# The first batch's depthwise convolution as five fp32 products on TensorE

## The chip, the cores and the metric

The kernel runs on one core of one Trainium2 chip, as one launch. The metric is the device time of one execution in microseconds; the median of several runs is compared. A core has five engines with an instruction queue each: TensorE (PE; its weight loads are shown as PEld), VectorE (DVE), ScalarE (ACT), GpSimd (POOL) and SyncE (SP).

## The reference

Three blocks follow one another: attention that keeps the 32 largest scores of a row, a gated layer whose gate is a causal depthwise convolution of five taps, and a mixer over tokens and channels. All data are float32.

```python
# attention: B, H, S, D = 4, 8, 576, 64
scores = q @ k.T / sqrt(D)
kth = 32nd largest of each row
attn = softmax(where(scores >= kth, scores, -1e9))
x = attn @ v                          # then to (4, 576, 512)
# gate: five taps a channel
xp = concatenate([zeros(4 rows), x])
gate_pre = sum(conv_w[k] * xp[:, k:k+S, :] for k in range(5))
gate = 1 / (1 + exp(-gate_pre))
x = (gate * (x @ w_val)) @ w_out
# mixer
theta = x @ w_theta
u = x + w_tok_r @ (x * cos(theta)) + w_tok_i @ (x * sin(theta))
out = u + maximum(u @ w_ch, 0)
```

## The kernel before

Channels lie on the 128 partitions and tokens along the free dimension in the gated layer. Two heads make a unit u (16 units: batch b = u // 4, head pair hp = u % 4). Attention works in 144 tiles of 128 query rows against 576 keys. In batch 0 (`SPLIT`) the units are gone through twice: first the query columns 0 to 255 of the four head pairs (x = 0, four tiles each), then columns 256 to 575 (x = 1, five tiles each). A stretch (u, x) is called a part here. In the other batches a unit's nine tiles are contiguous and its convolution is done once over 576 columns.

The main loop (L1317) takes one tile a step. In a step, VectorE picks the largest scores of one tile (`pick`), takes the threshold of an earlier one (`rest`) and masks a still earlier one (`mask`); ScalarE copies scores out of PSUM (`scores_out`), counts (`count`), exponentiates (`expo`) and copies the transposed tile (`turn_out`); GpSimd forms the products that the threshold needs (`below`); TensorE computes scores three tiles ahead (`scores_pe`, `AHEAD` = 3) and transposes (`turn`). VectorE and ScalarE execute in the order in which the program issues (`FIXED`); the framework's scheduler orders TensorE, GpSimd and the DMA queue by priority and readiness.

When the last tile of a part is masked, `close` starts a generator. `follow_up` resumes each such generator twice a step, so two yields are one step. It multiplies by v into `px` (L746), divides by the row sums into `xT` (L764), and then, from L788 on, convolves: tap 0 on ScalarE into g, tap 1 on ScalarE into `ct` and added by GpSimd, taps 2, 3 and 4 as multiply-adds on VectorE, and at last tanh in place (sigmoid is taken as tanh of half the argument). There are six yields between the first tap and tanh.

The gated layer and the mixer are jobs, generators in a list that is worked off in order: `front` (x @ w_val, gate, w_out, theta, sine and cosine) and `back` (token mix `py`, channel mix `ph`). In batch 0 `front` runs once for each half of the columns. Before each product with w_val it waits until the part's tanh is issued (`ready`). In each step `work` gives the jobs a budget in model nanoseconds, `BASE` = 4150; the attention's own TensorE work is taken from the same account `owed`, which can't be saved up beyond one step's amount. Batch 0 multiplies in plain fp32, later batches (`THREE`) in split halves.

PSUM tiles of `px`, the jobs and all that have tag "m" share four buffers (`ps_m`).

Of the kernel before, what the change touches and what calls it, by code (L numbers as in the profile page):

```python
# [11 lines left out]
F32 = mybir.dt.float32  # L12
# [4 lines left out]
AF = mybir.ActivationFunctionType  # L17
ALU = mybir.AluOpType
# [57 lines left out]
@with_exitstack  # L76
def attention_gate_phase_mixer(ctx, tc, *tensors):


    nc = tc.nc  # L80
    keep = ctx.enter_context(tc.tile_pool(name="keep", bufs=1))
    flag = keep.tile([1, 1], F32, name="flag")
    mixer(tc, *tensors, flag)

    over = nc.values_load(flag.bitcast(I32), min_val=0, max_val=0x7F000000,
                          skip_runtime_bounds_check_because="a count of rows")
    with tc.If(over > 0):
        mixer(tc, *tensors, None)
# [3 lines left out]
def mixer(ctx, tc, qT, kT, vt, w_val, conv_t, w_out, w_theta, w_tok, w_ch, out, flag):  # L92
    nc = tc.nc
    safe = flag is None
    P = 128
    B, S, DM = vt.shape
    U = qT.shape[0]
    NP = U // B
# [8 lines left out]
    NC = DM // P  # L107
    KW = conv_t.shape[1]
# [11 lines left out]
    ml = ctx.enter_context(tc.tile_pool(name="ml", bufs=1))  # L120
# [3 lines left out]
    ps_m = ctx.enter_context(tc.tile_pool(name="ps_m", bufs=BANKS[2], space=bass.MemoryType.PSUM))  # L124
# [39 lines left out]
    ident = cp.tile([P, P], F32, name="ident")  # L164
# [19 lines left out]
    raws, heads, there, ready = {}, {}, set(), set()  # L184
    s_tiles, s_psum, groups, xT, gate, W, ms = {}, {}, {}, {}, {}, {}, {}
    owed = [0.0]
# [5 lines left out]
    def tabled(out, src, func, **more):  # L192

        ins = nc.scalar.activation(out, src, func, **more).ins  # L194
        table = func == AF.Sin
        if (not table) in last and TABLED:
            tc.add_manual_dep(ins, last[not table].name, mybir.DependencyInfo(
                mybir.DependencyClass.NoSync, mybir.DependencyReason.DATA), reason="one table at a time")
        last[table] = ins
# [47 lines left out]
    def double(u, j, x):  # L247

        r = slice(64 * j, 64 * j + 64)
        q2 = q2s[j]  # L250
        kh, kl = (io.tile([P, S], I32, tag=f"{t}{j}", name=f"{t}{j}_{u}_{x}") for t in ("kh", "kl"))
        for d in range(2):
            o = slice(64 * d, 64 * d + 64)
            nc.sync.dma_start(kh[o, :], raws["k", u, x][0][r, :].bitcast(I32))
            nc.sync.dma_start(kl[o, :], raws["k", u, x][1][r, :].bitcast(I32))
            q = raws["q", u, x][d][r, :].bitcast(I32)
            c = columns_of("q", x)
            if j and c.stop == S:
                nc.sync.dma_start(q2[o, c.start : NF * P], q[:, c.start : NF * P])
                nc.sync.dma_start(q2[o, S:], q[:, NF * P :])  # L260
            else:
                nc.sync.dma_start(q2[o, c], q[:, c])
        heads[u, j] = tuple(t.bitcast(F32R) for t in (q2, kh, kl))
# [110 lines left out]
    ROOM = (CUT, S - CUT + REM)  # L374
# [303 lines left out]
    def turn_out(i):  # L678
# [5 lines left out]
        else:  # L684
            nc.scalar.copy(pT[:, e.j * NF : e.j * NF + NF, o : o + P], e.pt)  # L685

    def close(part):

        u, x = part["u"], part["x"]
        b, hp = divmod(u, NP)  # L690
        lo, hi = COLS[x]
        w = hi - lo
# [50 lines left out]
        for c in range(NF + 1):  # L743
            for j in range(2):
                r, k = (slice(0, P), j * NF + c) if c < NF else (slice(REM * j, REM * j + REM), 2 * NF)
                nc.tensor.matmul(px[64 * j : 64 * j + 64, :], v[r, c, 64 * j : 64 * j + 64], pT[r, k, :],  # L746
                                 start=(c == 0), stop=(c == NF), skip_group_check=True)
# [18 lines left out]
        split = b in SPLIT  # L766
        if not split and x == 0:
            return
        if split and x:
            g = gate[b][hp]  # L770
        else:
            drain(("gate", (u - GB) // NP))
            g = sp.tile([P, S], F32, tag="gp", name=f"gp_{u}", bufs=GB)
            gate.setdefault(b, []).append(g)
        if not split:
            lo = 0
        g = g[:, lo:hi]
# [7 lines left out]
        while lacking["conv"]:  # L785
            yield
            yield
        taps = [xt[:, k + lo : k + hi] for k in range(KW)]  # L788
        nc.scalar.activation(g, taps[0], AF.Copy, scale=cw[:, hp, 0:1])
        for k in CT:  # L790
            ct = wk.tile([P, S], F32, tag="ct", name=f"ct_{u}_{x}_{k}")[:, : g.shape[1]]
# [372 lines left out]
    for b in range(B):  # L1164
        late = b == B - 1
        f = 1.275 if b in THREE else 1.675
# [49 lines left out]
    for k, part in enumerate(order):  # L1216
        i0 = part["tiles"][0].i
        u, x = part["u"], part["x"]
        split = u // NP in SPLIT
# [4 lines left out]
        elif split or x == 0:  # L1224
            when = (i0 - 7, i0 - 5, i0 - 5, i0 - 4, i0 - 3) if split or i0 and order[k - 1]["x"] and order[k - 1]["u"] // NP in SPLIT else (i0 - 9, i0 - 8, i0 - 7, i0 - 6, i0 - 3)
            a = (u, x if split else None)
            for step, do in zip(when, (load_heads, split_high, split_low, *(
                    lambda u, x, j=j: double(u, j, x) for j in range(2)))):
# [37 lines left out]
    def begin_close(i):  # L1266
        e = seq[i]
        if e is e.part["tiles"][-1]:
            chains.append(close(e.part))
# [103 lines left out]
```

## Time and profile before

| | |
|---|---|
| median of 3 runs (lowest to highest) | 860.22 us (859.59 to 861.25) |
| profiled execution | 861.91 us |
| its span, first to last instruction | 859.8 us |
| busy: PE / DVE / ACT / POOL | 88% / 81% / 75% / 51% |
| mean granted TensorE clock | 0.938 |

The profile describes one execution. Busy times of an engine are shares of its span; a busy TensorE is one that has matmuls in flight, whose ends are modelled. A granted clock of 1.00 is 2.4 GHz, 0.50 is 1.2 GHz. The name before an arrow is what is written, the one behind it what is read; L801 is line 801 of the kernel. Most instructions overlap a neighbour a little at their ends, so start-to-start times are shorter than durations.

### The profile page before, as it was taken

The page shows a single profiled execution, that of the slowest core. Times are in us where ns is not written, and L with a number is a line of the kernel's source. Part 1 is how long each engine was busy: PE and PEld are TensorE (multiplying, and loading weights), DVE is VectorE, ACT ScalarE, POOL GpSimd, SP SyncE. Part 2 cuts the span into 40 slices and gives each one's busy share as a digit, 9 for nine tenths or more (in the row PEclk, how much of TensorE's full clock was granted, in tenths as well). Part 3 has the DMA queues.
Part 4 walks back from the last instruction along what each step waited for, and adds up shares of the span by engine and source line. Part 5 has one row for each costly group of instructions (what it writes and reads, how often), then busy time and mean ns, then how long its engine had stood idle before and what let it go on. Part 6 is the DMA issues. An engine that isn't in the chain of part 4 may idle for free.

```text
span 859.8 us, 15896 instructions
## 1 busy us (share of the span) xinstructions
PE 755.6 (88%) x4526; PEld 574.1 (67%) x4526; DVE 697.2 (81%) x2810; ACT 648.4 (75%) x1589; POOL 442.3 (51%) x579
## 2 busy tenths in 40 slices
PE   4577878958789598989798989999999999999995
PEld 3344556535555377668587677769797776798895
DVE  6999999989999769699988979889998696253522
ACT  6787898888888867697879789779888794436511
POOL 4766565655646335364758634546797143014500
PEclk9996888968999889999999989999999999999998
DMA  6576555634442214224755652222855300061002
GB/s 170 150 194 172 148 156 158 167 92 98 129 119 57 68 45 130 64 57 146 218 155 164 183 141 69 57 68 58 235 142 152 98 2 14 1 191 62 2 2 59
DMA packets 73601, 94.35 MB, mean 110 GB/s; under 512 B 13728, under 2 KB 37152, under 8 KB 73504
## 3 DMA queue, kind: packets, MB, share of 16 engines
q1 hardware_dynamic: 73184, 92.82, 39.8%
q8 instruction: 38, 0.62, 0.3%
q14 instruction: 59, 0.48, 0.2%
q10 hardware_dynamic: 320, 0.43, 0.2%
HBM read 49.96 MB, written 13.11 MB: 73 GB/s over the span
## 4 chain that ended last, share of the span: by engine, by line
PE 46%; DVE 33%; ACT 9%; issue 6%; POOL 4%; DMA 2%; SPq 0%; ACTq 0%; POOLq 0%; DVEq 0%
PE py L1087 10%; PE px L746 7%; DVE cand L573 7%; DVE thrs L600 5%; PE ph L508 5%; PE pth L508 4%; PE pt L666 3%; PE pval L508 3%; DVE gp L801 3%; PE py L1106 3%; DVE s L653 3%; DVE cand L579 3%; DVE tops L577 3%; PE px2t L508 2%; PE ps L537 2%
## 5 line engine op out<-in xcount | busy, mean ns | idle before, releaser
L594 POOL TENSOR_TENSOR y<-s,n 128x576 f32<-128x576 f32 x144 | 189.8, 1318 | 197.0 <-DVE thrs L600 148.2
L573 DVE MAX8 cand<-s 128x8 f32<-128x96 f32 x864 | 210.8, 245 | 0.5 <-ACT s L551 0.5
L653 DVE SCALAR_TENSOR_TENSOR s<-s,thrs,e 128x576 f32<-128x576 f32 x144 | 140.1, 973 | 8.0 <-ACT e L194 8.0
L586 ACT ACTIVATE n<-s,tops 128x576 bf16<-128x576 f32 x144 | 112.1, 778 | 34.2 <-POOL y L595 18.6
L551 ACT ACTIVATE s<-ps 128x256 f32<-128x256 f32 (+1 forms) x288 | 104.0, 406 | 41.3 <-PE ps L719 20.3
L666 PE MATMUL pt<-ident,s 128*128 128x128 f32 x576 | 97.9, 295 | 33.8 <-ACT pT L685 22.2
L746 PE MATMUL px<-pT,v 128*64 128x256 f32 (+3 forms) x640 | 111.5, 444 | 12.7 <-ACT pT L685 12.7
L1087 PE MATMUL py<-w_tok,z 128*128 128x256 f32 (+1 forms) x432 | 120.3, 421 | 1.7 <-DVE z L946 1.7
L600 DVE MAX8 thrs<-y 128x8 f32<-128x584 f32 x144 | 109.4, 759 | 6.3 <-POOL y L595 6.0
L666 PEld LDWEIGHTS pt<-ident,s 128*128 128x128 f32 x576 | 70.0, 148 | 62.8 <-ACT pT L685 32.2
L194 ACT ACTIVATE e<-s,least 128x576 f32<-128x576 f32 x144 | 110.8, 769 | 0.1
L537 PE MATMUL ps<-kh_None,q 128*128 128x256 f32 x240 | 95.9, 406 | 4.9 <-ACT s L551 2.9
L685 ACT COPY pT<-pt 128x512 f32<-128x512 f32 x128 | 73.1, 571 | 30.4 <-PE pt L666 18.6
L1087 PEld LDWEIGHTS py<-w_tok,z 128*128 128x128 f32 x432 | 80.9, 198 | 22.0 <-DVE z L946 2.5
L746 PEld LDWEIGHTS px<-pT,v 128*64 128x64 f32 (+1 forms) x640 | 44.6, 143 | 63.3 <-issue 28.0
L577 DVE MAX8 tops<-cand 128x8 f32<-128x48 f32 x432 | 83.0, 192 | 0.1
L538 PE MATMUL ps<-kl_None,q 128*128 128x256 f32 x240 | 72.9, 306 | 0.0
L537 PEld LDWEIGHTS ps<-kh_None,q 128*128 128x128 f32 x240 | 48.2, 201 | 24.2 <-issue 7.2
L537 PE MATMUL ps<-kh,q 128*128 128x256 f32 (+1 forms) x80 | 39.8, 502 | 19.1 <-ACT s L551 8.9
L579 DVE MATCH_REPLACE8 cand<-tops,cand 128x48 f32<-128x48 f32 x288 | 55.2, 192 | 0.0
L1066 DVE TENSOR_TENSOR x2T<-py,x2T 128x256 f32<-128x256 f32 (+1 forms) x32 | 14.4, 450 | 46.9 <-PE py L1087 27.8
L801 DVE SCALAR_TENSOR_TENSOR gp<-xT,w_conv,gp 128x576 f32<-128x576 f32 (+2 forms) x60 | 46.9, 782 | 6.0 <-POOL gp L793 5.3
(205 smaller groups left out, 1725.4 us busy)
## 6 DMA issues: line engine op xcount, KB each, us to landing
kh_None<-kh_None SPq DMA_DIRECT2D x48, 144.0 KB, 2.6
kl_None<-kl_None SPq DMA_DIRECT2D x48, 144.0 KB, 2.7
v<-in_vt_dram SPq DMA_DIRECT2D x20, 256.0 KB, 3.0
out_dram<-x2T SPq DMA_DIRECT2D x16, 256.0 KB, 3.1
w<-ch SPq DMA_DIRECT2D x16, 256.0 KB, 4.7
w<-theta SPq DMA_DIRECT2D x16, 256.0 KB, 5.1
raw_hi<-in_w_tok_dram SPq DMA_DIRECT2D x14, 256.0 KB, 2.8
kh<-kh SPq DMA_DIRECT2D x24, 144.0 KB, 2.4
```

Of the source, the lines that this page charges most:

```text
L194: ins = nc.scalar.activation(out, src, func, **more).ins
L508: nc.tensor.matmul(ps[o : o + n], x, y, start=(i + k == 0), stop=(i == last and k == len(ways) - 1), skip_group_check=(n < P))
L537: nc.tensor.matmul(bank[:, :w], q2, kh[:, lo:hi], start=(j == js[0]), stop=False)
L573: nc.vector.max(d["cand"][:, k, 8 * x : 8 * x + 8], s_tiles[i][:, x * SUB : (x + 1) * SUB])
L577: nc.vector.max(top, c)
L586: nc.scalar.activation(n, s_tiles[i], AF.Sign, bias=d["tops"][:, k, KC - 1 : KC], scale=-(1.0 + 2.0 ** -22), accum_out=acc)
L594: nc.gpsimd.tensor_tensor(y[:, :S], s_tiles[i], d.pop(("n", k)), ALU.mult)
L600: nc.vector.max(thrs[:, N - 1 - i : N - 1 - i + NK], d.pop(("y", k)))
L653: nc.vector.scalar_tensor_tensor(p, p, thr(i), e.exp, ALU.is_ge, ALU.mult, accum_out=part["sums"][:, e.slot : e.slot + 1])
L666: nc.tensor.transpose(e.pt[:, c, :], p[:, c * P : (c + 1) * P], ident)
L746: nc.tensor.matmul(px[64 * j : 64 * j + 64, :], v[r, c, 64 * j : 64 * j + 64], pT[r, k, :], start=(c == 0), stop=(c == NF), skip_group_che ...
L1087: nc.tensor.matmul(ps, z[:, m * P : (m + 1) * P], W["tok"][:, w, lo:hi], start=(i + k == 0), stop=(i == NF))
```

## The change

In batch 0 alone, each part's convolution becomes five fp32 matmuls that accumulate in one PSUM tile: the stationary operand of tap k is a 128 x 128 diagonal matrix of the tap's weights, the moving operand is `xT` shifted by k. Tanh reads PSUM and writes the gate. GpSimd makes the five diagonal matrices of a head pair in one operation (identity times taps, both broadcast) when a head pair is first met; they lie in a buffer with tag "room1" that batch 0 doesn't use until the second half of its `front`. The planner's account `owed` is charged 1.675 ns a column and tap. Between the matmuls and tanh there are two yields; the function returns before the old code.

```diff
--- before.py
+++ after.py
@@ -683,6 +683,19 @@
                            e.pt.rearrange("p c (j w) -> p j c w", j=2))
         else:
             nc.scalar.copy(pT[:, e.j * NF : e.j * NF + NF, o : o + P], e.pt)
+
+    diagonals = {}
+
+    def diagonal(hp):
+
+        if not diagonals:
+            all_of = ml.tile([P, 2 * NC * ROOM[1]], F32, tag="room1", name="diagonals")
+            diagonals["all"] = all_of[:, : NP * KW * P].rearrange("p (u k w) -> p u k w", u=NP, k=KW)
+        if hp not in diagonals:
+            diagonals[hp] = diagonals["all"][:, hp]
+            nc.gpsimd.tensor_tensor(diagonals[hp], ident.unsqueeze(1).broadcast_to([P, KW, P]),
+                                    W["conv"][:, hp, :].unsqueeze(2).broadcast_to([P, KW, P]), ALU.mult)
+        return diagonals[hp]
 
     def close(part):
 
@@ -786,6 +799,16 @@
             yield
             yield
         taps = [xt[:, k + lo : k + hi] for k in range(KW)]
+        if split:
+            owed[0] -= 1.675 * KW * (hi - lo)
+            ps = ps_m.tile([P, hi - lo], F32, tag="m", name=f"pconv_{u}_{x}")
+            for k in range(KW):
+                nc.tensor.matmul(ps, diagonal(hp)[:, k, :], taps[k], start=(k == 0), stop=(k == KW - 1))
+            yield
+            yield
+            tabled(g, ps, AF.Tanh, scale=0.5)
+            ready.add((u, x))
+            return
         nc.scalar.activation(g, taps[0], AF.Copy, scale=cw[:, hp, 0:1])
         for k in CT:
             ct = wk.tile([P, S], F32, tag="ct", name=f"ct_{u}_{x}_{k}")[:, : g.shape[1]]
```

## Rows read from the trace of the kernel before

**Rows 1.** Stretches, us: busy PE, PEld, DVE, ACT, POOL (instructions); clock; DMA share; GB/s.

```profile
60.00:245.00 185.00, 145.91 (x708) 95.13 (x709) 178.74 (x757) 158.18 (x419) 109.70 (x155) 0.82 0.53 138
245.00:285.00 40.00, 38.18 (x212) 22.96 (x211) 39.72 (x173) 34.53 (x91) 23.78 (x33) 1.00 0.33 81
285.00:302.00 17.00, 9.38 (x59) 5.42 (x60) 12.62 (x54) 16.09 (x32) 4.95 (x8) 0.83 0.35 85
302.00:425.00 123.00, 113.31 (x695) 88.27 (x694) 105.06 (x441) 95.47 (x236) 63.01 (x77) 0.95 0.39 107
425.00:760.00 335.00, 324.60 (x2096) 255.09 (x2097) 271.94 (x1090) 261.39 (x630) 180.02 (x218) 0.98 0.37 103
```

**Rows 2.** Waits of VectorE and ScalarE, 60 to 245 us: total us, times, longest.

```profile
DVE s L653 <- ACT e L194: 3.6, 2, 3.4
DVE xT L764 <- ACT rb L726: 1.1, 1, 1.1
...
ACT pT L685 <- PE px L746: 11.7, 4, 4.0
```

**Rows 3.** Instruction groups, 60 to 245 us: busy us, mean ns, idle before.

```profile
L653 DVE SCALAR_TENSOR_TENSOR s<-s,thrs,e 128x576 f32<-128x576 f32 x37 | 34.6, 935 | 3.6 <-ACT e L194 3.6
...
L801 DVE SCALAR_TENSOR_TENSOR gp<-xT,w_conv,gp 128x320 f32<-128x320 f32 x12 | 7.5, 625 | 0.1
...
L801 DVE SCALAR_TENSOR_TENSOR gp<-xT,w_conv,gp 128x256 f32<-128x256 f32 x12 | 6.7, 558 | 0.1
...
L793 POOL TENSOR_TENSOR gp<-gp,ct 128x320 f32<-128x320 f32 x4 | 3.5, 866 | 0.0
...
L793 POOL TENSOR_TENSOR gp<-gp,ct 128x256 f32<-128x256 f32 x4 | 3.2, 803 | 0.0
...
L789 ACT ACTIVATE gp<-xT,w_conv 128x320 f32<-128x320 f32 x4 | 2.2, 557 | 0.0
...
L789 ACT ACTIVATE gp<-xT,w_conv 128x256 f32<-128x256 f32 x4 | 2.0, 492 | 0.0
```

**Rows 4.** Timeline: a mask alone, and one beside an add on GpSimd.

```profile
61.84 0.81 DVE L653 SCALAR_TENSOR_TENSOR s<-s,thrs,e 128x576 f32<-128x576 f32 x1
...
69.86 0.87 POOL L793 TENSOR_TENSOR gp<-gp,ct 128x256 f32<-128x256 f32 x1
...
70.06 1.28 DVE L653 SCALAR_TENSOR_TENSOR s<-s,thrs,e 128x576 f32<-128x576 f32 x1
```

**Rows 5.** Timeline of TensorE: fp32 products, 256 columns at both clocks, 320 at full.

```profile
102.04 2.32 PE L508 MATMUL pval<-xT,w_val 128*128 128x256 f32 x10
...
146.16 2.76 PE L508 MATMUL px2t<-gp,w_out 128*128 128x256 f32 x6
...
260.95 2.32 PE L508 MATMUL px2t<-gp,w_out 128*128 128x320 f32 x8
```

**Rows 6.** Stretches of 2 us as in the first group, with the granted clock.

```profile
66.00:68.00 2.00, 0.85 (x4) 0.45 (x2) 1.97 (x7) 2.00 (x5) 0.56 (x2) 0.50 0.87 250
...
74.00:76.00 2.00, 1.86 (x16) 0.70 (x12) 2.00 (x15) 0.01 (x1) 1.43 (x2) 0.95 0.35 121
...
146.00:148.00 2.00, 2.00 (x7) 1.64 (x6) 2.00 (x12) 1.96 (x7) 1.20 (x2) 0.50 0.29 60
```

**Rows 7.** Timeline: the last part of batch 0 and the jobs around it.

```profile
189.62 2.48 DVE L946 TENSOR_TENSOR z<-px,z 128x512 f32<-128x512 f32 x4
...
223.38 0.48 DVE L764 TENSOR_TENSOR xT<-px,rb 128x320 f32<-128x320 f32 x1
...
227.80 0.59 ACT L789 ACTIVATE gp<-xT,w_conv 128x320 f32<-128x320 f32 x1
...
244.80 0.46 ACT L194 ACTIVATE gp<-gp 128x320 f32<-128x320 f32 x1
...
248.96 0.45 DVE L830 SCALAR_TENSOR_TENSOR gp<-gp,pval 128x320 f32<-128x320 f32 x1
...
302.25 1.06 PE L1087 MATMUL py<-w_tok,z 128*128 128x256 f32 x2
```

## The prediction

> **What bounds the kernel now.** I read the stage table first [rows 1]: busy time of every engine in five stretches, with the granted clock behind it. Between 60 and 245 us VectorE is busy 178.7 of 185 us (97%), ScalarE 158.2, TensorE only 145.9. From 302 us on it is the other way round: TensorE holds 113.3 of 123 us, then 324.6 of 335, while VectorE falls to about 80%. So there are two regimes: VectorE paces the attention of the first batch, TensorE everything after it. Between them, at 285 to 302, TensorE idles 7.6 of 17 us. All eight convolutions that the diff touches lie in the first regime.
>
> The table of waits [rows 2] confirms it: VectorE has two kinds of wait worth a row in these 185 us, together 4.7 us, of which 3.4 is one mask waiting for an exponential. ScalarE, however, waited 11.7 us in four goes for its transposed tiles, which stood behind the attention products px on TensorE; that did not reach VectorE then, because the kernel computes scores three tiles ahead.
>
> **What is removed.** Per part of 256 or 320 columns there go two copies on ScalarE (L789, L792), one add on GpSimd (L793) and three multiply-adds on VectorE (L801). VectorE: 12 multiply-adds of 256 columns, 6.7 us, and 12 of 320, 7.5 us [rows 3], together 14.2. One part, the second half of head pair 1, lies in 170 to 200 us, where two table loads and the sines sit on ScalarE and VectorE has its only long wait; its three, a quarter of 7.5 = 1.9, I count at nothing. That leaves 12.3 us. ScalarE: four groups of copies, 2.2 + 2.0 for L789 and the same again for L792, 8.4 us; ScalarE has 27 us of room, so at nothing; were it the pace setter, up to 8.4 us more.
>
> **What is added on GpSimd.** Four products of 5 x 128 = 640 elements, one for each head pair. No row has this shape. The adds take 803 ns for 256 and 866 ns for 320 elements [rows 3]; continued along this slope 640 cost 1.2 us, in proportion to the smaller one 2.0. I take 1.6, so 6.4 us, against eight adds removed: 4 x 0.80 + 4 x 0.87 = 6.7. Net nothing. GpSimd is busy 109.7 of 185 us, and the products need only the identity and the taps, so they can fill its gaps; the first matmul of a head pair waits for its product at worst, 1.6 us four times, behind which scores stand that are wanted only three tiles later.
>
> A GpSimd operation can also hold VectorE up: a mask that takes 0.81 us alone took 1.28 beside an add [rows 4], 0.47 us more. Eight such delays leave, four perhaps longer ones come: from -3.8 us to, if each product stops VectorE for its whole length, +6.4. I take 0, since the GpSimd time is equal.
>
> The Trainium skill, SBUF — State Buffer, section "Who interferes with whom", speaks against the new products: VectorE and GpSimd share a port pair under an exclusive lock, and the loser blocks to the end. The 0.47 us agree with it. By the strict rule the sum below would lose up to 6.4 us and stand at about 856; by the equal times it stands as worked out.
>
> **What is added on TensorE.** Five fp32 products a part. An fp32 product leaves two records: 10 records of 256 columns took 2.32 us, 8 of 320 took 2.32 [rows 5], so about 0.21 and 0.27 us each once neighbours overlap, 0.43 and 0.53 a product. (The last of a merged row still drains, so the row divided by its count is a little high.) A part costs 5 x 0.43 = 2.13 or 2.67 us, eight parts 4 x 4.8 = 19.2 us at 2.4 GHz. At 1.2 GHz six records of 256 took 2.76 us [rows 5], twice as much: 38.4 is the upper end. The clock is down in places: 0.50 at 66 to 68 us after thin work, back at 0.95 by 74 to 76 after a stretch of products [rows 6]; the mean of the stage is 0.82, so 19.2 / 0.82 = 23.4 us at today's clock. The idle time there is 185 - 145.9 = 39.1 us [rows 1]. It fits, but TensorE comes to 169.3 of some 173. Lower bound of what this costs: 0, all in gaps; upper: 39.1 us of gaps are there, half of them waits that stay, so up to 23.4 - 19.5 = 4 us beyond the old pace. I take 2 us off the gain, as the row that is nearest (four waits of ScalarE behind px, at most 4.0 us [rows 2]) did not reach VectorE.
>
> The Trainium skill, TensorE: Matmul & The Clock Gate, Part 1, says that the slow clock is the default and activity lifts it. The clock rows agree; by it the added work would cost nearer 19.2 than 23.4 us, which favours the sum as it stands.
>
> **What moves.** The generator yields twice instead of six times between the first tap and tanh. On the last part tanh stands at 244.80 us, 17 us after the first tap at 227.80, and the last gating product at 248.96 waits for it [rows 7]. Two yields are a step of about 5 us (37 masks in 185 us [rows 3]), so tanh comes two steps earlier. Against that, each part takes 2.14 or 2.68 us off the planner's budget `owed`, 19.3 in all, so other jobs are emitted later. I put both at zero together: the first half's jobs reach their last product at 189.62 us and the second half's begin after 223.38 [rows 7], so the debits of most parts fall where nothing waits, and the last one (2.68 us, a step of spare budget) is about what the earlier tanh gives back.
>
> The accumulator takes one of four buffers of `ps_m` until tanh has read it, a step; px behind it could wait for one; that is part of the 2 us above and of C below. Tanh reads PSUM instead of SBUF; no row has that, bounds 0 and a doubling of 8 x 0.46 = 3.7 us on ScalarE, below the 8.4 it sheds.
>
> **Sum.** 12.3 - 2 = 10.3 us. The profiled execution took 861.9 (span 859.8 and 2.1 around it), so 851.6; the median of the runs shown is 860.2, 1.7 lower, so **850** for that. Bounds: with all 14.2 us and 3.8 of port delays and no contention, 842; with 6.4 of port delays and 4 of contention, 860.2 - 12.3 + 10.4 = 858.
>
> **The rivals.** B: the earlier tanh does more. If the second half's chain moves up a step or two, the token mix that starts at 302.25 us [rows 7] fills the 7.6 us that TensorE idles before it, and the TensorE regime starts sooner: 850 - 7.6 = 842. For it speaks that the gate is the last thing waited for; against, the last debit.
>
> C: TensorE becomes the bound of the first regime. 169.3 us of work plus a quarter to a half of the present gaps (9.8 to 19.5) is 179 to 189 us against 185: 854 to 864, middle 859. For it: px already holds ScalarE up by 4.0 us once. Against: three tiles of lead.
>
> D, slower: the debited budget pushes other jobs out of the VectorE regime, where they cost nothing, past 302 us, where TensorE is full. All 19.3 us there less 12.3 gained gives +7, 867. It decides as soon as more than 12.3 us end there. Against: the pause from 190 to 223 us, which takes up seven of the eight debits.
>
> **How the numbers follow.** My forecast 0.50, B 0.15, C 0.20, D 0.10, other 0.05. A measurement of this kernel tells about 0.2% (1.7 us) from no change. Faster: forecast, B, half of C and a little of the rest, 0.77; same 0.07, from C; slower: D, the upper part of C and the rest, 0.16. The range reaches from below B's centre, 840, to most of C, 863; the forecast's own is 842 to 858.
>
> **What would show it.** VectorE's busy time in the first regime falls by about 14 us, and it stays at 95% or more while the tile steps there get shorter; TensorE's rises by 19 to 23; the token mix starts about 10 us sooner (B: 15 or more) and the span after it is unchanged. The prediction is wrong if VectorE shows new waits for ScalarE or for px (C), if the token mix starts earlier but takes longer to its end (D), or if masks beside the new GpSimd products grow by more than they did.

## The result, and the profile after

The changed kernel takes 850.83 us in the median (849.82 to 853.01), 0.989 of the kernel before [0.987, 0.991]: about 9.5 us faster. 850 was forecast, 10.2 below. The total was right; two of its terms were wrong, by about 5 us each, and cancelled. The profiled execution of the changed kernel was the slowest of its four, 853.01 us.

The stages of the changed kernel, columns as in [rows 1]. The first two are cut at the same times as there, the others at the start of the token mix:

```profile
60.00:245.00 185.00, 161.12 (x844) 110.12 (x844) 173.80 (x778) 161.37 (x430) 107.03 (x159) 0.88 0.57 147
245.00:285.00 40.00, 37.01 (x194) 22.49 (x192) 37.97 (x167) 34.47 (x85) 23.46 (x32) 0.91 0.25 61
285.00:294.00 9.00, 5.43 (x36) 3.25 (x36) 4.62 (x15) 8.89 (x18) 0.56 (x1) 0.88 0.57 139
294.00:417.00 123.00, 113.38 (x695) 87.95 (x693) 105.27 (x443) 95.27 (x236) 63.27 (x77) 0.95 0.39 108
417.00:751.00 334.00, 322.88 (x2093) 253.52 (x2094) 271.06 (x1089) 261.69 (x629) 180.49 (x218) 0.98 0.37 102
```

The token mix starts at 294.01 us, 8.2 earlier than before [rows 7]. From there on the kernels are alike: 113.38 of 123 us on TensorE against 113.31, and then the same again [rows 1]. The span is 851.1 against 859.8, so 8.2 of the 8.7 us are won before the token mix. In the first regime TensorE is busy 161.1 us instead of 145.9, and its clock rose from 0.82 to 0.88. VectorE is now idle for 11 of 185 us, before for 6, and says why:

```profile
DVE s L653 <- ACT e L194: 4.2, 1, 4.2
DVE xT L777 <- ACT rb L739: 2.9, 3, 1.3
DVE z L931 <- ACT z L924: 2.0, 1, 2.0
DVE gp L853 <- PE pval L508: 0.7, 1, 0.7
```

There were two kinds of wait before [rows 2], together 4.7 us; these four add up to 9.8 us. Two of them, for a theta copy and for a job's product, are new. ScalarE's own wait for px, 11.7 us before, did not fall:

```profile
ACT pT L685 <- PE px L759: 12.0, 5, 3.3
```

The new operations, first in groups (60 to 245 us), then in the timeline:

```profile
L806 PE MATMUL pconv<-xT,diagonals 128*128 128x320 f32 x40 | 14.2, 503 | 0.4 <-DVE xT L777 0.4
...
L806 PE MATMUL pconv<-xT,diagonals 128*128 128x256 f32 x40 | 12.8, 480 | 0.8 <-DVE rs L711 0.8
```

```profile
220.54 2.32 PE L806 MATMUL pconv<-xT,diagonals 128*128 128x320 f32 x8
```

```profile
20.70 2.47 POOL L696 TENSOR_TENSOR diagonals<-ident,w_conv 128x640 f32<-128x640 f32 x2
25.27 1.45 POOL L594 TENSOR_TENSOR y<-s,n 128x576 f32<-128x576 f32 x1
26.84 2.47 POOL L696 TENSOR_TENSOR diagonals<-ident,w_conv 128x640 f32<-128x640 f32 x2
29.95 1.79 POOL L594 TENSOR_TENSOR y<-s,n 128x576 f32<-128x576 f32 x1
```

```profile
26.92 0.77 DVE L600 MAX8 thrs<-y 128x8 f32<-128x584 f32 x1 [1.33 <-POOL y L595]
29.43 1.17 DVE L653 SCALAR_TENSOR_TENSOR s<-s,thrs,e 128x576 f32<-128x576 f32 x1
...
56.14 0.81 DVE L653 SCALAR_TENSOR_TENSOR s<-s,thrs,e 128x576 f32<-128x576 f32 x1
```

The four GpSimd products are not spread over 60 to 110 us, where their first use is. The scheduler issues them as soon as the taps are there, between 20.7 and 29.3 us, ahead of the products that the thresholds need. VectorE waits 1.33 us for its threshold's input, and the mask behind it takes 1.17 us instead of 0.81 [rows 4]. Two more of its operations there take longer than in the kernel before: L325 0.83 us instead of 0.43, and L330 behind the mask 1.36 instead of 0.28. Together this is 3.2 us. The seventh mask of the kernel before:

```profile
52.40 0.81 DVE L653 SCALAR_TENSOR_TENSOR s<-s,thrs,e 128x576 f32<-128x576 f32 x1
```

In the changed kernel it stands at 56.14: 3.7 us are lost before the first convolution, and about 12 gained from there to 250 us.

### The profile page after: what moved, and what is told of

It reads as the page before. It is cut to its first block, busy times and chain, and to the rows that moved or that the text cites. A ratio compares the mean times of both kernels' runs of the same rounds, so it can differ in the third digit from the quotient of the medians.

```text
span 851.1 us, 16006 instructions
## 1 busy us (share of the span) xinstructions
PE 761.0 (89%) x4606; PEld 583.3 (69%) x4606; DVE 680.6 (80%) x2786; ACT 641.6 (75%) x1573; POOL 437.9 (51%) x575
## 4 chain that ended last, share of the span: by engine, by line
PE 53%; DVE 26%; ACT 8%; POOL 5%; issue 4%; DMA 3%; SPq 0%; ACTq 0%; POOLq 0%; DVEq 0%
PE py L1110 9%; PE px L759 9%; DVE cand L573 6%; PE ph L508 5%; PE pth L508 5%; PE px2t L508 4%; DVE thrs L600 4%; PE pval L508 4%; PE pt L666 4%; PE ps L537 3%; PE py L1129 3%; DVE s L653 3%; PE ps L538 2%; DVE cand L579 2%; DVE gp L824 2%
## 5 line engine op out<-in xcount | busy, mean ns | idle before, releaser
L759 PE MATMUL px<-pT,v 128*64 128x256 f32 (+3 forms) x640 | 106.4, 432 | 9.4 <-ACT pT L685 9.4
L666 PE MATMUL pt<-ident,s 128*128 128x128 f32 x576 | 95.6, 289 | 20.8 <-ACT pT L685 11.6
L537 PE MATMUL ps<-kh_None,q 128*128 128x256 f32 x240 | 93.5, 397 | 6.5 <-ACT s L551 5.2
L537 PE MATMUL ps<-kh,q 128*128 128x256 f32 (+1 forms) x80 | 37.9, 479 | 20.8 <-ACT s L551 9.6
L538 PEld LDWEIGHTS ps<-kl_None,q 128*128 128x128 f32 x240 | 47.4, 197 | 2.9 <-issue 0.7
```

Source lines behind the costliest of these rows:

```text
L537: nc.tensor.matmul(bank[:, :w], q2, kh[:, lo:hi], start=(j == js[0]), stop=False)
L538: nc.tensor.matmul(bank[:, :w], q2, kl[:, lo:hi], start=False, stop=(j == js[-1]))
L666: nc.tensor.transpose(e.pt[:, c, :], p[:, c * P : (c + 1) * P], ident)
```

## Experiments

Times are medians, each with its ratio to runs of the kernel before on the same chip and a 95% interval; those runs had medians of 860.5 to 861.3. "Ahead" and "behind" are the start of the same mask in two profiled executions. Waits and clocks are those of 60 to 245 us in one profiled execution.

**GpSimd products alone.** The kernel before, with `diagonal` issued and never read.

```diff
+        if split:
+            diagonal(hp)
         nc.scalar.activation(g, taps[0], AF.Copy, scale=cw[:, hp, 0:1])
```

> The kernel before, with the four GpSimd products added at the place where the changed kernel has them; nothing reads them, the old convolution stays. Theory: the masks fall 3.7 us behind in the first 30 us and stay there, 864 us. Rival (the early delay is taken back by idle time later, and the gain of the change is simply 10): 860.7.

863.68 us, 1.0026 [1.0017, 1.0035]. The masks are 3.4 us behind at the fourth and 4.2 at 250 us, as expected; less than all of it reaches the end. The products cost 2.2 us.

**Products held back.** The changed kernel, with the products issued at the closing of each head pair's first part.

```diff
+            tc.add_manual_dep(ins, evicted[0].name, mybir.DependencyInfo(
+                mybir.DependencyClass.Sync, mybir.DependencyReason.SCHED_ONLY), reason="not in the start")
...
+        if b in SPLIT and not lacking["conv"]:
+            diagonal(hp)
```

> The changed kernel, with each of the four GpSimd products held back until the closing of its head pair's first part. Theory (the products cost 3.3 to 3.7 us because they are issued between 20 and 30 us, where VectorE waits for GpSimd, and the VectorE relief itself is worth 12): the seventh mask comes at about 52.5 us instead of 56.1 and the time falls by 3 us to 847.5. Rival (a product costs the same wherever it stands, since VectorE is just as full later): the delay moves to 50 to 110 us, and the time stays at 851.

850.61 us, 0.988 [0.987, 0.990], not to be told from the changed kernel. The fourth mask is only 0.1 us behind that of the kernel before instead of 3.7, but the tenth is 2.1 behind: a microsecond for each of the two products issued by then. The theory that only their early place costs fell; the rival holds, within the interval. (At 250 us this profiled execution is 2 us ahead of the changed kernel's; the medians do not show that.)

**No debit.**

```diff
-            owed[0] -= 1.675 * KW * (hi - lo)
```

> The changed kernel without the charge to the planner's account. Theory (the debits fall where the account has nothing to spend): 851, within 2 us. Rival (the debits push jobs past 300 us, where TensorE is full): up to 19 us of TensorE work comes forward, and the time falls to 840 to 846. Third: without the charge VectorE's and ScalarE's queues meet products that TensorE has not finished, and the time rises by 2 to 5 us.

849.69 us, 0.987 [0.985, 0.988]: 1 us less by the medians, 2 by the ratios, with intervals that overlap. The debits are not what holds the kernel back.

**Six yields before tanh.**

```diff
-            yield
-            yield
+            for _ in range(6):
+                yield
             tabled(g, ps, AF.Tanh, scale=0.5)
```

> The changed kernel with tanh issued six yields after the products, as in the kernel before, instead of two. Theory (the gain is VectorE's relief alone): 851, within 2 us. Rival (the gate is what the second half's chain waits for, and the two steps bring part of the gain): the token mix starts 5 to 8 us later than in the changed kernel, and the time is 855 to 859.

846.45 us, 0.983 [0.981, 0.985]: 5 us faster than with two yields, where my theory said the same and the rival slower. The token mix starts at 289.2 us, 4.8 earlier than with two yields, not later. The rows of the changed kernel that show a place of it, then those of this one:

```profile
160.96 0.81 DVE L653 SCALAR_TENSOR_TENSOR s<-s,thrs,e 128x576 f32<-128x576 f32 x1
161.87 0.59 ACT L685 COPY pT<-pt 128x512 f32<-128x512 f32 x1 [2.29 <-PE px L759]
...
163.74 0.69 ACT L924 ACTIVATE z<-pth,magic 128x512 f32<-128x512 f32 x1
164.46 0.69 DVE L931 SCALAR_TENSOR_TENSOR z<-z,pth 128x512 f32<-128x512 f32 x1 [2.02 <-ACT z L924]
...
167.58 0.81 DVE L653 SCALAR_TENSOR_TENSOR s<-s,thrs,e 128x576 f32<-128x576 f32 x1
```

```profile
158.53 0.59 ACT L685 COPY pT<-pt 128x512 f32<-128x512 f32 x1 [2.02 <-PE px L759]
158.96 0.81 DVE L653 SCALAR_TENSOR_TENSOR s<-s,thrs,e 128x576 f32<-128x576 f32 x1
...
162.87 0.81 DVE L653 SCALAR_TENSOR_TENSOR s<-s,thrs,e 128x576 f32<-128x576 f32 x1
...
168.31 0.69 ACT L924 ACTIVATE z<-pth,magic 128x512 f32<-128x512 f32 x1
169.16 0.68 DVE L931 SCALAR_TENSOR_TENSOR z<-z,pth 128x512 f32<-128x512 f32 x1
```

Both times px holds ScalarE up for two microseconds. With two yields the theta copy (L924) stands behind that wait in the same step, its partner L931 is the instruction that VectorE waits at, and the next mask comes 6.6 us after the last one (167.58). With six yields the theta copy is two steps later, nothing of that step on VectorE waits for ScalarE, and the mask comes after 3.9 us. Here the gain can be seen. In the whole stretch ScalarE waits less for px with six yields (12.0 us with two), at the same mean clock of 0.88:

```profile
ACT pT L685 <- PE px L759: 6.9, 4, 2.2
```

VectorE's waits fall with it, from 9.8 us to 5.1, which is about the gain. That all of it is of the kind shown here is argued, not shown.

**No multiply-adds.** The kernel before without L801 in batch 0.

```diff
         for k in rest:
-            nc.vector.scalar_tensor_tensor(...)
+            if not split:
+                nc.vector.scalar_tensor_tensor(...)
```

> The kernel before without VectorE's 24 multiply-adds of batch 0 (taps 2 to 4 are left out of its gate); order and yields as before, nothing added on TensorE or GpSimd. Theory (VectorE's relief is worth its busy time, 12.3 us): 861 - 12 = 849, the masks 12 us ahead by 250 us. Rival (the relief alone is worth less, part of the changed kernel's gain comes from ScalarE and GpSimd): 853 to 857. Third (it is worth more, and the products on TensorE take part of it away): 841 to 846.

855.05 us, 0.994 [0.992, 0.995]: only 5.5 us for 14.2 us of VectorE's time, in the rival's range. The stage, ScalarE's longest wait and VectorE's:

```profile
60.00:245.00 185.00, 146.59 (x743) 95.48 (x744) 170.88 (x759) 163.06 (x434) 110.64 (x161) 0.84 0.54 141
```

```profile
ACT pT L685 <- PE px L746: 16.2, 5, 4.4
...
DVE s L653 <- ACT e L194: 5.1, 2, 4.9
DVE xT L764 <- ACT rb L726: 3.3, 4, 1.1
DVE cand L573 <- ACT s L551: 2.6, 2, 1.4
DVE z L909 <- ACT z L902: 1.9, 1, 1.9
```

VectorE catches up with ScalarE, which stands behind px for 16.2 us (before 11.7 [rows 2]), and waits 12.9 us itself.

**Everything added, nothing removed.** The old convolution, and beside it the GpSimd and the TensorE products with the debit, unread.

> The kernel before with the four GpSimd products and the forty fp32 products on TensorE added, with the charge to the planner's account; nothing reads their result, the old convolution stays. The kernel with the GpSimd products alone took 863.7. Theory (the fp32 products lie in TensorE's gaps): 864 to 866. Rival (they collide with the attention's products, which ScalarE then waits for): 868 to 875, with waits of ScalarE for px well above the 11.7 us of before.

860.73 us, 1.000 [0.998, 1.0015]. Nineteen microseconds of TensorE work and four GpSimd products cost nothing. The theory's 864 was too high, the collision did not come: the clock of the stage is 0.88, and ScalarE waits 3.2 us for px instead of 11.7. So I measured the TensorE work by itself.

**TensorE work alone.** Kernel before, or the kernel without multiply-adds, plus:

```diff
+        if split:
+            owed[0] -= 1.675 * KW * (hi - lo)
+            ps = ps_m.tile([P, hi - lo], F32, tag="m", name=f"pconv_{u}_{x}")
+            for k in range(KW):
+                nc.tensor.matmul(ps, ident, taps[k], start=(k == 0), stop=(k == KW - 1))
         nc.scalar.activation(g, taps[0], AF.Copy, scale=cw[:, hp, 0:1])
```

> The kernel before with the same unread products (identity as stationary operand) and nothing else changed. Theory (more work on TensorE holds the clock up; together with the GpSimd products it took 860.7, the GpSimd products alone 863.7, so the fp32 products are worth -3): 858. Rival (VectorE paces these stages at any clock): 861. Third (19 us more work on an engine that later is the bound): 865 or more.

857.96 us, 0.997 [0.995, 0.999], as the theory had it: unread work makes the kernel faster. The clock is 0.88, ScalarE waits 3.2 us for px and VectorE 1.3 in all.

> The kernel without the 24 multiply-adds (taps 2 to 4 left out, 855.1), with five fp32 products a part added on TensorE, the identity as stationary operand, result unread; nothing added on GpSimd, the old copies, the add and the yields stay. Theory (the added products hold the clock up, px then delays ScalarE less, and only so VectorE's relief pays in full): mean clock of 60 to 245 us 0.88 instead of 0.84, waits of ScalarE for px under 10 us instead of 16, and 846 to 850. Rival (the rest of the changed kernel's gain comes from the copies and adds that it takes off ScalarE and GpSimd): 855 to 858, for TensorE only gets more work.

844.50 us, 0.982 [0.981, 0.984]: the same unread work takes 9.7 us off the kernel without multiply-adds by the ratios, 10.6 by the medians. Stage and waits:

```profile
60.00:245.00 185.00, 164.10 (x851) 111.23 (x851) 180.21 (x793) 170.46 (x452) 114.64 (x166) 0.90 0.56 149
```

```profile
ACT pT L685 <- PE px L746: 4.7, 4, 2.1
...
DVE s L653 <- ACT e L194: 3.4, 1, 3.4
```

The clock is 0.90 instead of 0.84, ScalarE's wait for px fell from 16.2 to 4.7 us, VectorE's from 12.9 to 3.4, and VectorE is busy 180.2 of 185 us again. As the theory had it, and a little more. One px group shows what the clock does. First the kernel without multiply-adds, then this one: the same twenty products and the ScalarE copy that waits behind them.

```profile
72.68 3.84 PE L746 MATMUL px<-pT,v 128*64 128x256 f32 x20
...
76.64 0.59 ACT L685 COPY pT<-pt 128x512 f32<-128x512 f32 x1 [4.45 <-PE px L746]
```

```profile
71.62 2.53 PE L746 MATMUL px<-pT,v 128*64 128x256 f32 x20
...
74.28 0.58 ACT L685 COPY pT<-pt 128x512 f32<-128x512 f32 x1 [2.07 <-PE px L746]
```

From the group's start to the copy the granted clock is 0.66 in the first and 1.00 in the second. Of the 16.2 us that ScalarE waits for px without the added products, 10.9 lie in stretches with a clock of 0.56 to 0.74; the other 5.4 came at 1.00, so they are not the clock's. The edit carries the debit and shifts the scheduler's order on TensorE too; the debit removed alone made nothing slower above, and the share of the order is not separated.

**No convolution at all.** Copies, add and multiply-adds of batch 0 left out, tanh of the first tap's data after six yields.

> The kernel before with the whole convolution of batch 0 left out: tanh of the first tap's data after six yields, no copies, no GpSimd add, no multiply-adds, no products. If the copies and the GpSimd add matter (rival of the clock theory): 849 or less, for all is taken away. If the clock matters: TensorE idles even more, the clock stays at 0.84 or below, and the time is 853 to 856, slower than the changed kernel although it does less.

846.52 us, 0.984 [0.983, 0.986]. Here my clock theory missed: I expected 853 to 856. The clock is 0.84 and ScalarE waits 16.7 us for px, as expected, yet it is 8.5 us faster than the kernel without multiply-adds. So at the low clock the copies on ScalarE and the GpSimd add do cost; which of them is open. The prediction had priced the copies at up to 8.4 us if ScalarE should set the pace. Even so it is no faster than the kernel with copies, add and unread products (844.50).

**Better versions.** Late products with six yields; then diagonals made by ScalarE; then those with ten yields.

```diff
-            nc.gpsimd.tensor_tensor(diagonals[hp], ...)
+            for k in range(KW):
+                nc.scalar.activation(diagonals[hp][:, k, :], ident, AF.Copy, scale=W["conv"][:, hp, k : k + 1])
```

> The changed kernel with the GpSimd products held back until the closing and with six yields before tanh. If the two effects are separate (six yields gave 4.4 us, holding back gave nothing in time but 3.6 us in the first 60): 845 to 847, as with six yields alone. If holding back is worth its 2 to 3 us when the later collisions are gone: 843.

846.87 us, 0.984 [0.982, 0.986]: as six yields alone.

> As the kernel with late products and six yields, but the diagonal matrices are made by ScalarE, five copies of 128 columns with the tap as scale for each head pair, at the closing of the first part. ScalarE has room there and shares nothing with VectorE's queue. Theory (a GpSimd product costs about 1 us wherever it stands, because VectorE's two-input operations wait beside it): 3 to 4 us less than the six-yield kernel, 843. Rival (the products' delay is hidden later anyway): 846. Third (ScalarE, at over 18 of 20 us in places, passes its 5 us on): 848 to 850.

845.27 us, 0.982 [0.980, 0.984]: 1.8 us less than with late GpSimd products, not beyond the intervals.

> The kernel with ScalarE-made diagonals (845.3), with ten yields before tanh instead of six. If a later tanh always spares VectorE waits: 842. If six are enough and the gate is the next thing waited for: two steps later in the second half's chain, 848 to 852.

837.63 us, 0.973 [0.972, 0.975], the fastest version: 13 us below the changed kernel. "A later tanh always helps" is closer than "six are enough", but not by my reason. Up to 306 us this kernel is 13.0 us ahead of the kernel before, less than the one with six yields and ScalarE-made diagonals (15.7), and VectorE's waits in the first regime are no fewer. Its token mix starts at 296.4 us, 10 later than there. It gains afterwards: at 445 us it is 24.8 ahead against 19.9, with the clock at 0.99 instead of 0.96 from 300 to 420 us. Why, these runs do not settle.

## Why the prediction was right, and where not

The single changes make a path from the old kernel to the changed one. Steps are differences of ratios times 860.7, each uncertain by some 2.5 us.

| step | ratio | measured | forecast |
|---|---|---|---|
| fp32 products on TensorE (unread) | 0.997 | -2.7 | +2 |
| multiply-adds off VectorE | 0.982 | -12.6 | -12.3 |
| GpSimd products in, copies and add out | 0.983 | +0.6 | 0 |
| two yields instead of six | 0.989 | +5.2 | 0 |
| sum | | -9.5 | -10.3 |

That the total came within 1 us is luck: TensorE's products were priced about 5 us too high and the earlier tanh about 5 us too low. The shares also hold for this order of steps alone. Taken off first, the multiply-adds are worth 5.5 us, and the TensorE products then 9.7.

The waits go with the times (60 to 245 us, one profiled execution each):

| kernel | clock | ScalarE for px, us | VectorE in all, us | median, us |
|---|---|---|---|---|
| before | 0.82 | 11.7 | 4.7 | 860.2 |
| unread products added | 0.88 | 3.2 | 1.3 | 858.0 |
| no multiply-adds | 0.84 | 16.2 | 12.9 | 855.1 |
| the same, unread products added | 0.90 | 4.7 | 3.4 | 844.5 |
| changed | 0.88 | 12.0 | 9.8 | 850.8 |
| changed, six yields | 0.88 | 6.9 | 5.1 | 846.5 |

**VectorE paces the first regime.** Right, and its price too, on one condition that the prediction did not see. With the TensorE products there (clock 0.88 to 0.90) the multiply-adds are worth 12.6 us, without them (0.82 to 0.84) 5.5, for then VectorE runs into ScalarE's waits for px. The prediction had read that wait and left it out, as three tiles of lead had hidden it so far.

**TensorE's products.** The duration at full clock was right: eight records of 320 columns took 2.32 us, as in [rows 5]. In all the groups were busy for 27.0 us, not 19.2 or 23.4, as some still ran at a granted clock of 0.54 to 0.74. The sign of the cost was wrong. I took 2 us for collisions; added alone, the products lie in gaps, the granted clock of the stage rises from 0.82 to 0.88, and px delays ScalarE less (3.2 us instead of 11.7). The clock stood in [rows 6], and I used it to lower a cost when it was a gain of its own. The rule of the Trainium skill, TensorE: Matmul & The Clock Gate, Part 1, that activity lifts the slow clock, pointed this way; the three pairs of runs agree with it (0.82 to 0.88 twice, 0.84 to 0.90 once).

The clock is not all of it. In the changed kernel, at 0.88, ScalarE still waits 12.0 us for px, and 9.3 of them lie in stretches with a granted clock of 1.00. One of them:

```profile
134.75 3.05 PE L759 MATMUL px<-pT,v 128*64 128x320 f32 x18
...
137.93 0.59 ACT L685 COPY pT<-pt 128x512 f32<-128x512 f32 x1 [3.30 <-PE px L759]
```

Here a whole px group stands in front of the transposes that ScalarE's copy needs. With six yields this wait is 0.8 us: the group comes in pieces there, with only the last, 1.44 us, in front of the copy. Rival C, TensorE as the bound, fell: TensorE has 24 of 185 us idle.

**GpSimd products.** A product took 1.25 us, near the lower bound of 1.2, not 1.6. Against the removed adds and copies they come to nothing, as forecast, but alone they cost 2.2 us, and I placed them in gaps where the scheduler had no reason to put them. The strict reading of the port rule in the Trainium skill, SBUF — State Buffer, "Who interferes with whom" (6.4 us), is too high for the time: the loss of 2.2 us holds waits for the threshold's input besides any port delay.

**The earlier tanh.** This step failed. I set the two steps' gain and the debit against each other at zero, and rival B even expected a gain. It costs 5.2 us. At the place shown, the theta copy comes forward into a step where px blocks ScalarE, and VectorE executes in order. The token mix started 8.2 us earlier, not the 15 of B. That tanh reads PSUM cost nothing, as taken: 0.41 to 0.42 us for 320 columns, 0.45 to 0.48 from SBUF before.

**Budget (rival D).** Fell: the stages from the token mix on are unchanged, and without the debits the time moves by 1 to 2 us, within the intervals.

**The signs.** The token mix came sooner and the span after it is unchanged, as said. From the ninth mask to the 45th the kernel before takes 181.7 us, the changed one 169.5; VectorE's busy time falls from 175.5 to 158.5 us there, its share from 97% to 93%, below the 95% named. TensorE's busy time in 60 to 245 us rises by 15 us, not 19 to 23. The new wait of VectorE for ScalarE, 2.0 us at a theta copy, was named as a sign of C; it stands at the place shown above and is gone with six yields.

## What to carry to other kernels

When an engine's share is taken off the path, look at what it waits for once it is faster: here matmul groups in front of ScalarE, mostly at a lowered clock, took more than half of the gain, and work added to TensorE gave it back. An operand's early readiness is enough for a scheduler to issue it early; look for where a new operation will be issued, not where it is first used. And in queues of fixed order, an instruction that is ready sooner should not therefore be issued sooner: try the issue distance as a parameter of its own.

## What the runs showed of the hardware that was not expected

Forty unread fp32 products (about 19 us of TensorE time) made an execution 2.7 us shorter, and one with less work on VectorE about 10 us shorter; the granted clock of the stage rose with them by 0.06 both times.
